# First batch's transform kept in SBUF, weights converted by VectorE, first loads placed by hand

## Chip, core and metric

The kernel runs on one core of a Trainium2 chip. The metric is device time in microseconds (us) of one launch, the median of several runs; lower is better.

## What is computed

Three stages follow one another. `x` has 8 batches of 3072 rows with 256 columns, float32.

```
X = np.fft.rfft(x, axis=1); y = np.fft.irfft(X * (filt_r + 1j * filt_i), n=3072, axis=1)
h = y @ w_in                        # 256 -> 1024, y as 24576 rows
sm = softmax(h); solu = h * sm
ln = (solu - mean) / sqrt(var + 1e-6) * g_ln
z = ln @ w_out                      # 1024 -> 256
h2 = z @ w_in2                      # 256 -> 2048
out = (h2 * sigmoid(1.702 * h2)) @ w_out2    # 2048 -> 256
```

The four weight matrices are float64 in memory and are turned into float32 on the chip.

## The kernel before

**Filter.** The Fourier transform of a batch is two matrix products. In the first (`step1`), rows are taken with a stride of 24, so that a tile has 128 partitions; a batch has 12 such tiles of 128 x 512 (`load_x`, `step1`, `store_a`). The result `a` goes to DRAM (`a_d`). In the second, 32 groups of 96 rows (`NG`) are read back (`load2`: 96 KB of `bt` from `a_d`, 264 KB of `gt` with the group's matrices and filter), multiplied (`forward`, `swap`), filtered (`weigh`), turned back (`inverse`) and stored to DRAM (`z_d`, `store_z`). Batch 0 runs alone through `EarlyFilter`, with one float32 matmul for each product; batches 1 and 2 and later ones run in pairs, mixed into the other stages' work.

**Two layers.** 96 pairs of 128-row tiles go through `First` (filter's last product, 256 -> 1024, softmax, norm, a shuffle through DRAM, 1024 -> 256) and `Second` (256 -> 2048, tanh gate, 2048 -> 256). The first `First` reads `z_d` of batch 0 and so needs all 32 groups of it (`assert filtered[b] == NG`).

**Weights.** 24 parts of 128 x 512 float64 words (512 KB each) are loaded (`Weights.load`) and converted: on VectorE (DVE) `magnitude` (3 instructions), `sign` (1), `lower` (2); on GpSimd (POOL) `add`; on ScalarE (ACT) `scale_rows` for some parts and `split_hi`; on POOL `split_lo`. Fifteen parts (`EARLY["count"]`) are converted along with batch 0's filter, in two buffers (tag "e"); nine (w4's and one more) after it, in three.

**Order.** Nothing is scheduled by the compiler. Each step is put into a list with a time (`at`), the list is sorted, and each engine and the one DMA queue (SyncE, SP) take their instructions in that order; 16 units are one pair. The tables `FIRST`, `SECOND`, `DENSE`, `EARLY` hold the times. An instruction that waits holds up all that stand behind it on its engine, and a DMA issue that waits for a free buffer holds up all later DMA issues.

```
start2 = end - v["gap"] - step2 * NG        # first group of batch 0
start1 = start2 - step1 * N2 / 2            # first step1 of batch 0
steps = (f.load2, f.split_m, f.split_a, f.forward, f.swap, f.weigh, f.split_y, f.inverse, f.store_z)
```

Of the kernel before, what the change touches and what calls it, by code (L numbers as in the profile page):

```python
# [10 lines left out]
F32 = mybir.dt.float32  # L11
F32R = mybir.dt.float32r
# [5 lines left out]
ALU = mybir.AluOpType  # L18
# [5 lines left out]
B, S, D = 8, 3072, 256  # L24
# [12 lines left out]


FIRST = {
    "load": -18.49,  # L40
    "y": -15.7,
    "y_lo": -15.4,
    "hidden": ((-13.6, -11.51), (-5.09, -3.6)),
    "top": (-10.5, -2.4),
    "exp": (-9.6, -1.76),
    "weigh": (-8.86, -1.07),
    "square": (-7.25, 0.3),
    "norm": (-6.23, 0.53),
    "shuffle": (-5.5, 1.2),
    "gather": (-4.48, 1.94),  # L50
    "turn": (-1.56, 6.83),
    "u_hi": (-0.97, 7.3),
    "u_lo": (-0.15, 8.0),
    "project": ((9.4, 10.4), (11.4, 12.1)),
    "x2_hi": 12.78,
    "x2_lo": 13.6,
}
# [1 line left out]
SECOND = {  # L59
    "tanh": 0.7,  # L60
    "gate": 1.19,
    "split_hi": 2.42,
    "split_lo": 3.19,
    "output": 4.6,
    "finish": 5.0,
    "store": 6.2,
}


# [7 lines left out]
DENSE = {  # L77
    "start": 15.65,
    "slots": (0.77, 4.65, 8.65, 12.36),
    "second": (-6.99, -2.67, -1.85, -0.07, 0.61, 5.46, 7.59, 10.78, 11.33),  # L80
}

EARLY = {
    "end": -37.0,
    "step1": 0.99,
    "step2": 1.04,
    "gap": 3.8,
    "first": (-2.8, -2.1, 0.0, 0.5),
    "second": (0.7, 1.6, 1.0, 2.8, 2.95, 3.1, 3.35, 4.6, 5.3),
    "direct": 20,  # L90
    "wide": 8,
    "count": 15,
    "between": 4,
    "ahead": ((0.5, 1.6), (1.4, 1.5)),
    "weights": ((-0.7, 1.6), (-3.5, 4.0)),
    "weight": ((-4.9, -2.9, -1.5, -0.6, 0.2, 1.4, 1.8, 2.4), (-1.7, -1.6, -0.6, -0.4, 0.6, 0.9, 1.6, 1.8)),
}


# [88 lines left out]
def fft_filter_solu_gelu(  # L188
# [62 lines left out]
    def split_pair(k, n, name):  # L251
        hi = cst.tile([P, k, n], F32R, name=f"{name}_hi")
        lo = cst.tile([P, k, n], F32R, name=f"{name}_lo")
        return hi, lo
# [1 line left out]
    w1 = split_pair(2, FF1, "w1")  # L256
    w2 = split_pair(K1, D, "w2")
    w3 = split_pair(2, FF2, "w3")
    w4 = split_pair(K2, D, "w4")

    staged = []

    class Weights:


        def __init__(self, n, dst, src, gain, k0, kn, c0, cn):
            self.hi, self.lo = (t[:, k0:k0 + kn, c0:c0 + cn] for t in dst)
            self.shape = [P, kn, cn]
            k, c = slice(k0, k0 + kn), slice(c0, c0 + cn)
            self.half = dst is w4  # L270
            if gain is None:
                self.src = [(slice(0, P), src.rearrange("(k p) n -> p k n", p=P)[:, k, c])]
            else:
                self.src = [
                    (part, rows.rearrange("(k f) n -> f k n", f=Q)[:, k, c])
                    for part, rows in (blocks(src, b) for b in range(P // Q))]
            self.n, self.gain, self.k0 = n, gain, k0

        def load(self):
            if self.n < EARLY["count"]:  # L280
                self.raw = p2.tile(self.shape, U64, tag="e", name="wst")
            else:

                if self.n == EARLY["count"]:
                    staged.append(p1.tile([P, 3, 512], U64, tag="x2", name="wst"))
                self.raw = staged[0][:, self.n % 3].rearrange("p (k n) -> p k n", k=self.shape[1])
            for part, src in self.src:
                dma(out=self.raw[part], in_=src)

# [30 lines left out]
                op0=ALU.mult, op1=ALU.mult)  # L320

        def add(self):
            nc.gpsimd.tensor_tensor(self.f, self.f, self.top.bitcast(F32), op=ALU.add)
            self.f = self.f.rearrange("p (k n) -> p k n", k=self.shape[1])

        def scale_rows(self):
# [13 lines left out]
                        out=self.f[:, k], in_=self.f[:, k], func=AF.Copy, scale=g)  # L340

        def split_hi(self):
            nc.scalar.copy(out=self.hi, in_=self.f)

        def split_lo(self):
            nc.gpsimd.tensor_tensor(self.lo, self.f, self.hi, op=ALU.subtract)

    def weight_parts():
        n = 0
# [16 lines left out]
    def at(t, fn, *args):  # L366
        plan.append((t, len(plan), fn, args))

    def in_order(*times):
        assert all(a < b for a, b in zip(times, times[1:])), times  # L370
# [13 lines left out]
    filtered = [0] * B  # L384

    class Filter:
        pools = {"gt": [(p3, "gt")], "bt": [(p3, "bt")]}

        def __init__(self, batches):
            b0, self.nb = batches[0], len(batches)  # L390
# [15 lines left out]
        def load_x(self, i0):  # L406
            b, i = divmod(i0, N2 // 2)
            xv = x[self.batches[b]].rearrange("(m q) d -> m (q d)", q=N2)
            if self.batches[0] == 0 and i0 < EARLY["wide"]:

                if i0 == 0:
                    self.wide = p1.tile([N1, EARLY["wide"], 2 * D], F32, tag="u", name="xin")
                xt = self.wide[:, i0]
            else:
                xt = p2.tile([N1, 2 * D], F32, tag="xin", name="xin")
            dma(out=xt, in_=xv[:, i * 2 * D:(i + 1) * 2 * D])
            self.x[i0] = xt
# [5 lines left out]
        def step1(self, i):  # L423
            f = ps_m.tile([N1, 2 * D], F32, tag="m", name="f1")
            if i < self.direct:
                nc.tensor.matmul(f, dft1_sb[:, 0], self.x.pop(i), start=True, stop=True)
            else:
                product(f, (fwd1[:, 0], fwd1[:, 1]), self.x.pop(i))
            self.a[i] = p2.tile([N1, 2 * D], F32, tag="az", name="a")
            nc.scalar.copy(out=self.a[i], in_=f)  # L430

        def store_a(self, i):
            b, j = divmod(i, N2 // 2)
            av = self.a_d[b].rearrange("g r d -> (g r d)").rearrange("(s f) -> s f", s=N1)
            dma(out=av[:, j * 2 * D:(j + 1) * 2 * D], in_=self.a.pop(i))
            self.stored += 1

        def load2(self, g):
            assert self.stored == self.steps
            bt = self.tile("bt", g, [R, self.nb, D], F32)  # L440
            dma(out=bt, in_=self.a_d[:, g].rearrange("b r d -> r b d"))
            gt = self.tile("gt", g, [R, 2 * R + 2 * D], F32)
            dma(out=gt, in_=groups[:, g])
            fl = gt[:, 2 * R:].rearrange("p (t n) -> p t n", t=2)
            both = [R, self.nb, D]
            self.t[g] = dict(
                bt=bt, m=gt[:, :2 * R],
                fr=fl[:, 0:1].to_broadcast(both), fi=fl[:, 1:2].to_broadcast(both))

        def split_m(self, g):  # L450
# [48 lines left out]
    class EarlyFilter(Filter):  # L499


        pools = {"gt": [(p3, "gt")], "bt": [(p3, "bt")] * 3 + [(p2, "xs")] * 2}
        wide_gt = None

        def tile(self, name, g, shape, dtype):
# [40 lines left out]
        def inverse(self, g):  # L546
            v = self.t[g]
            f = ps_m.tile([R, self.nb, D], F32, tag="m", name="f3")
            nc.tensor.matmul(f, v["m"][:, R:], v["pr"], start=True, stop=True)
            v["z"] = p2.tile([R, self.nb, D], F32, tag="az", name="z")  # L550
            nc.scalar.copy(out=v["z"], in_=f)

    def plan_filter(batches, first, second):

        f = Filter(batches) if batches[0] else EarlyFilter(batches)
        for i in range(f.steps):
            in_order(*first(i))
            for t, step in zip(first(i), (f.load_x, f.split_x, f.step1, f.store_a), strict=True):
                at(t, step, i)
        for g in range(NG):  # L560
            steps = (
                f.load2, f.split_m, f.split_a, f.forward, f.swap, f.weigh, f.split_y, f.inverse,
                f.store_z)
            t = second(g)
            in_order(t[0], *t[2:])
            in_order(t[0], t[1], t[3])
            for t, step in zip(second(g), steps, strict=True):
                at(t, step, g)

# [276 lines left out]
    for k, block in enumerate(BLOCKS):  # L848
# [4 lines left out]
    start2 = end - v["gap"] - step2 * NG  # L853
    start1 = start2 - step1 * N2 / 2
    plan_filter(
        together[0], lambda i: [start1 + step1 * i + d for d in v["first"]],
        lambda g: [start2 + step2 * g + d for d in v["second"]])

    def dense(g):
        p, k = divmod(g, len(DENSE["slots"]))  # L860
# [2 lines left out]
    def ahead(i):  # L863
        (a, b), (c, d) = v["ahead"]
        n = v["between"]
        t = start2 + a + b * i if i < n else end + c + d * (i - n)
        return [t + dt for dt in v["first"]]

    plan_filter(together[1], ahead, dense)
    for batches in together[2:]:  # L870
# [4 lines left out]
        def second(g):  # L875

            t = piece(len(batches) * N2 // 2 + 4 * (g // 2) + g % 2)
            return [t + d for d in FILTER["second"]]

        plan_filter(batches, lambda i: [piece(i - 4) + d for d in FILTER["first"]], second)  # L880
    for i, w in enumerate(weight_parts()):
        (a, b), (c, d) = v["weights"]
        n = EARLY["count"]
        t = start1 + a + b * i if i < n else end + c + d * (i - n)
        steps = (
            w.load, w.magnitude, w.sign, w.lower, w.add, w.scale_rows, w.split_hi, w.split_lo)
        in_order(*v["weight"][i < n])
        for d, step in zip(v["weight"][i < n], steps, strict=True):
            at(t + d, step)
# [43 lines left out]
```

## Time and profile before

| what | us |
|---|---|
| median of 3 runs | 3744.72 (3741.65 to 3746.28) |
| profiled execution, its own time | 3743.48 |
| span of its trace | 3741.6 |
| first load of x issued, from the span's start | 3.57 |
| first load of `bt` issued | 51.67 |
| last store of batch 0's `z_d` issued | 148.78 |
| first matmul of `Second` (L765) | 248.50 |

The span runs from the first to the last recorded instruction. PE is TensorE's matmul row, PEld its weight loads, SPq the issuing of DMAs on SyncE's queue. "DMA share" is the mean busy share of the core's 16 DMA engines. In the chain of waits, a piece "DMA x<-y" is time in which the next instruction waited for that transfer.

### The profile page before, as it was taken

The numbers are of one execution on the slowest core, as the hardware profiler recorded it, in microseconds if no ns is written. First come the engines' busy times: TensorE is split into PE (matmuls) and PEld (weight loads), VectorE is DVE, ScalarE is ACT, GpSimd is POOL, SyncE is SP. The second block draws the span as 40 slices with busy tenths as digits, with TensorE's granted clock in tenths as the row PEclk, the third lists the DMA queues.
The fourth block names the chain that finished last, engine by engine and source line by source line (L and its number), as shares of the span: only waits on it lengthen the run. The fifth ranks groups of instructions, "written<-read, shape, count | busy, mean of one in ns | idle before, by whom it ended". The sixth has DMA issues, their size and how long they took to land.

```text
span 3741.6 us, 53627 instructions
## 1 busy us (share of the span) xinstructions
PE 3633.5 (97%) x18304; PEld 3017.0 (81%) x18304; DVE 2691.7 (72%) x3825; ACT 1998.7 (53%) x3570; POOL 860.0 (23%) x1397
## 2 busy tenths in 40 slices
PE   5779999999999999999999999999999999999999
PEld 2368888888888888888888888888888888888888
DVE  8658887667777777666777777667777776766675
ACT  2246665555555555555555555555555554544453
POOL 4333332222222221222222222122222221111110
PEclk6889999999999999999999999999999999999999
DMA  7745554334434443343434343433333332222321
GB/s 225 229 149 152 149 151 123 124 121 114 115 114 114 116 119 104 124 135 108 118 111 122 109 118 112 115 110 102 107 110 106 101 107 86 76 80 72 87 74 32
DMA packets 385683, 433.93 MB, mean 116 GB/s; under 512 B 144128, under 2 KB 294784, under 8 KB 385408
## 3 DMA queue, kind: packets, MB, share of 16 engines
q1 hardware_dynamic: 385408, 430.49, 39.6%
q8 instruction: 145, 2.38, 0.3%
q14 instruction: 130, 1.06, 0.1%
HBM read 232.13 MB, written 176.16 MB: 109 GB/s over the span
## 4 chain that ended last, share of the span: by engine, by line
PE 83%; DVE 7%; DMA 3%; issue 3%; POOL 1%; ACT 1%; SPq 1%; DVEq 0%; POOLq 0%; ACTq 0%
PE h L765 24%; PE o L804 24%; PE x L706 15%; PE h L624 12%; PE f L382 5%; PE yt L606 2%; DVE e L649 1%; DVE u L696 1%; DVE th L777 1%; SPq L827 1%; DMA wst<-in_w_in 1%; POOL mt L454 1%; DVE ob L815 1%; DMA xw<-xs 1%; DMA e_d<-e 0%
## 5 line engine op out<-in xcount | busy, mean ns | idle before, releaser
L765 PE MATMUL h<-x2s,w_hi 128*128 128x512 f32 (+1 forms) x3136 | 956.5, 387 | 0.0
L783 ACT CAST gh<-th 128x512 fp32r<-128x512 f32 x768 | 474.2, 617 | 465.1 <-DVE th L777 386.3
L777 DVE SCALAR_TENSOR_TENSOR th<-th,h 128x512 f32<-128x512 f32 x768 | 523.8, 682 | 246.0 <-ACT th L772 242.8
L789 DVE TENSOR_TENSOR gl<-th,gh 128x512 fp32r<-128x512 f32 x768 | 534.6, 696 | 194.7 <-ACT gh L783 192.2
L765 PEld LDWEIGHTS h<-x2s,w_hi 128*128 128x128 f32 x3136 | 571.7, 189 | 107.6
L772 ACT ACTIVATE th<-h 128x512 f32<-128x512 f32 x768 | 457.5, 596 | 335.2 <-PE h L765 334.7
L706 PE MATMUL x<-u,w_hi 128*128 128x256 f32 x3072 | 622.9, 285 | 11.6 <-DVE u L696 10.5
L804 PE MATMUL o<-gh,w_hi 128*128 128x512 f32 (+1 forms) x1568 | 615.9, 393 | 2.0 <-DVE ob L815 1.7
L804 PE MATMUL o<-gl,w_hi 128*128 128x512 f32 (+1 forms) x1568 | 607.4, 387 | 0.0
L804 PE MATMUL o<-gh,w_lo 128*128 128x512 f32 (+1 forms) x1568 | 606.6, 387 | 0.0
L706 PEld LDWEIGHTS x<-u,w_hi 128*128 128x128 f32 x3072 | 505.8, 192 | 37.2 <-DVE u L696 18.8
L765 PE MATMUL h<-x2s,w_lo 128*128 128x512 f32 (+1 forms) x1568 | 478.3, 386 | 0.0
L706 PE MATMUL x<-u,w_lo 128*128 128x256 f32 x1536 | 435.8, 284 | 0.0
L636 ACT ACTIVATE e<-h,nmx 128x1024 f32<-128x1024 f32 x192 | 214.6, 1117 | 326.1 <-DVE nmx L630 309.9
L804 PEld LDWEIGHTS o<-gl,w_hi 128*128 128x128 f32 x1568 | 295.0, 188 | 68.9 <-DVE gl L789 9.6
L804 PEld LDWEIGHTS o<-gh,w_hi 128*128 128x128 f32 x1568 | 296.1, 189 | 63.8 <-issue 11.0
L765 PEld LDWEIGHTS h<-x2s,w_lo 128*128 128x128 f32 x1568 | 292.8, 188 | 62.5
L804 PEld LDWEIGHTS o<-gh,w_lo 128*128 128x128 f32 x1568 | 296.1, 189 | 51.0
L640 POOL TENSOR_SCALAR q<-se 128x1 f32<-128x1 f32 x192 | 44.1, 230 | 1204.8 <-ACT e L636 1204.7
L706 PEld LDWEIGHTS x<-u,w_lo 128*128 128x128 f32 x1536 | 294.6, 192 | 14.9
L669 DVE TENSOR_SCALAR e<-e,nmu,rs 128x1024 f32<-128x1024 f32 x192 | 160.8, 837 | 179.8 <-POOL rs L664 177.4
L649 DVE SCALAR_TENSOR_TENSOR e<-h,e 128x1024 f32<-128x1024 f32 x192 | 232.2, 1209 | 33.3 <-ACT e L636 20.7
(82 smaller groups left out, 5303.0 us busy)
## 6 DMA issues: line engine op xcount, KB each, us to landing
e_d<-e SPq DMA_DIRECT2D x192, 512.0 KB, 2.6
e<-e_d SPq DMA_DIRECT2D x768, 128.0 KB, 3.0
gt<-in_groups SPq DMA_DIRECT2D x160, 264.0 KB, 3.8
xin<-in_x SPq DMA_DIRECT2D x96, 256.0 KB, 3.3
a_d<-a SPq DMA_DIRECT2D x96, 256.0 KB, 2.3
zr<-z_d SPq DMA_DIRECT2D x96, 256.0 KB, 3.3
out<-ob SPq DMA_DIRECT2D x768, 32.0 KB, 1.6
bt<-a_d SPq DMA_DIRECT2D x96, 192.0 KB, 3.5
```

Of the source, the lines that this page charges most:

```text
L382: nc.tensor.matmul(out, w[i], x[j], start=m == 0, stop=m == 2)
L624: nc.tensor.matmul(hs, xx[:, c, a * P:(a + 1) * P], ww[:, c, f * 512:(f + 1) * 512], start=(m == 0 and c == 0), stop=(m == 2 and c == 1))
L636: nc.scalar.activation(out=e, in_=self.h[a], func=AF.Exp, bias=self.v[a], accum_out=se)
L649: nc.vector.scalar_tensor_tensor(out=e, in0=self.h[a], scalar=1.0, in1=e, op0=ALU.mult, op1=ALU.mult, accum_out=su)
L669: nc.vector.tensor_scalar(out=e, in0=e, scalar1=nmu, scalar2=rs, op0=ALU.add, op1=ALU.mult)
L706: nc.tensor.matmul(self.x2[:, c], ww[:, kk, c * P:(c + 1) * P], uu[:, kk], start=(c == 0 and kk == 0 and m == 0), stop=(kk == K1 - 1 and m ...
L765: nc.tensor.matmul(self.part(t, j), ww[:, c, f * P:(f + 1) * P], xx[..., c, :], start=(m == 0 and c == 0), stop=(m == 2 and c == 1))
L772: nc.scalar.activation(out=th, in_=self.t[d], func=AF.Tanh, scale=0.851)
L777: nc.vector.scalar_tensor_tensor(out=self.g[d], in0=self.g[d], scalar=1.0, in1=self.t.pop(d), op0=ALU.add, op1=ALU.mult)
L783: nc.scalar.copy(out=gh, in_=self.g[d])
L789: nc.vector.tensor_tensor(gl, th, gh, op=ALU.subtract)
L804: nc.tensor.matmul(o, ww[:, f, h * P:(h + 1) * P], self.part(gg, j), start=(f == 0 and m == 0), stop=(f == K2 - 1 and m == 2))
```

## The change

- The 12 tiles of batch 0's x are loaded first, with three weight parts among them, into one tile `x0` of 24 KB per partition, which takes the place in SBUF that w4's converted weights take later. `step1` writes its result back into `x0`; `store_a` does nothing for batch 0.
- `load2` falls into `load_gt` and `load_bt`. For batch 0 `load_bt` copies SBUF to SBUF: 24 rows of 1 KB from each of the four partitions `4g` to `4g+3` to the 96 partitions of `bt`. `load_gt` of the first eight groups stands earlier, beside `step1`.
- `add` and `split_lo` of the weights go from POOL to DVE.
- Weight parts 0 to 14 use five buffers instead of two; each load has a time of its own (`loads`).
- Batch 0's `z` has six buffers instead of two.
- Some times in `FIRST`, `SECOND` and `DENSE` move by up to about one unit.

```diff
 EARLY = {
     "end": -37.0,
-    "step1": 0.99,
-    "step2": 1.04,
-    "gap": 3.8,
-    "first": (-2.8, -2.1, 0.0, 0.5),
-    "second": (0.7, 1.6, 1.0, 2.8, 2.95, 3.1, 3.35, 4.6, 5.3),
+    "step1": 0.73,
+    "step2": 0.95,
+    "gap": 2.88,
+    "x": (-3.0, 0.1),
+    "gt": (-0.01, 1.11),
+    "first": (-2.1, 0.0, 0.5),
+    "second": (0.3, 0.31, 1.19, 1.3, 2.52, 2.82, 3.47, 4.1, 4.6, 5.3),
...
+    "loads": (-81.75, -81.7, -81.86, -77.86, -75.86, -73.86, -71.86, -69.86, -67.86, -65.86, -63.86, -61.86, -59.86, -57.86, -55.86, -46.4, -42.4, -38.4, -34.96, -30.4, -26.12, -22.4, -18.4, -16.17),
-    "weights": ((-0.7, 1.6), (-3.5, 4.0)),
+    "weights": ((1.12, 1.9), (-3.5, 4.0)),
...
+    x0 = p1.tile([N1, N2 // 2, 2 * D], F32, tag="w4", name="x0")
...
-            if self.n < EARLY["count"]:
+            if self.n < EARLY["count"] and self.n % 5 > 2:
                 self.raw = p2.tile(self.shape, U64, tag="e", name="wst")
             else:
...
-                self.raw = staged[0][:, self.n % 3].rearrange("p (k n) -> p k n", k=self.shape[1])
+                self.raw = staged[0][:, STAGE[self.n]].rearrange("p (k n) -> p k n", k=self.shape[1])
...
         def add(self):
-            nc.gpsimd.tensor_tensor(self.f, self.f, self.top.bitcast(F32), op=ALU.add)
+            nc.vector.tensor_tensor(self.f, self.f, self.top.bitcast(F32), op=ALU.add)
...
         def split_lo(self):
-            nc.gpsimd.tensor_tensor(self.lo, self.f, self.hi, op=ALU.subtract)
+            nc.vector.tensor_tensor(self.lo, self.f, self.hi, op=ALU.subtract)
...
-            self.a[i] = p2.tile([N1, 2 * D], F32, tag="az", name="a")
+            if self.batches[0] == 0:
+
+                nc.scalar.copy(out=x0[:, i], in_=f)
+                self.stored += 1
+                return
+            self.a[i] = self.tile("az", i, [N1, 2 * D], F32)
             nc.scalar.copy(out=self.a[i], in_=f)
 
         def store_a(self, i):
+            if self.batches[0] == 0:
+                return
...
+        def load_bt(self, g):
             assert self.stored == self.steps
             bt = self.tile("bt", g, [R, self.nb, D], F32)
-            dma(out=bt, in_=self.a_d[:, g].rearrange("b r d -> r b d"))
+            if self.batches[0] == 0:
+                dma(out=bt[:, 0],
+                    in_=x0[4 * g:4 * g + 4].rearrange("s a (b d) -> s (a b) d", d=D))
+            else:
+                dma(out=bt, in_=self.a_d[:, g].rearrange("b r d -> r b d"))
...
-        pools = {"gt": [(p3, "gt")], "bt": [(p3, "bt")] * 3 + [(p2, "xs")] * 2}
+        pools = {
+            "gt": [(p3, "gt")], "bt": [(p3, "bt")] * 3 + [(p2, "xs")] * 2,
+            "az": [(p2, "az"), (p2, "fh"), (p2, "fl")] * 2}
...
+        lambda g: (
+            start1 + v["gt"][0] + v["gt"][1] * g if g < 8
+            else start2 + step2 * g + v["second"][0]))
```

## Rows read from the trace of the kernel before

**Rows 1.** The page, busy share of each engine, then 40 slices.
```profile
PE 3633.5 (97%) x18304; PEld 3017.0 (81%) x18304; DVE 2691.7 (72%) x3825; ACT 1998.7 (53%) x3570; POOL 860.0 (23%) x1397
PE   5779999999999999999999999999999999999999
```

**Rows 2.** Busy time by stage: us of stretch, us and count by engine.
```profile
core 0: us, PE busy (x) PEld busy (x) DVE busy (x) ACT busy (x) POOL busy (x), PEclk, DMA share, GB/s
0.00:51.70 51.70, 26.12 (x28) 7.14 (x28) 40.47 (x53) 15.55 (x30) 20.35 (x20) 0.66 0.75 232
51.70:149.00 97.30, 68.79 (x200) 36.33 (x198) 77.31 (x147) 18.75 (x45) 37.76 (x81) 0.74 0.75 217
149.00:300.00 151.00, 114.88 (x537) 86.48 (x536) 89.56 (x124) 69.48 (x128) 53.49 (x68) 0.83 0.56 173
300.00:3700.00 3400.00, 3389.38 (x17304) 2855.12 (x17305) 2466.67 (x3475) 1881.10 (x3348) 748.38 (x1228) 1.00 0.38 110
```

**Rows 3.** Chain of waits from 0 to 149 us, share by line.
```profile
by line: DMA wst<-in_w_in 16.1%; DMA gt<-in_groups 10.4%; DVE w_top L310 7.9%; DVE w_mag L301 7.4%; issue 6.1%; PE f L549 6.1%; PE f L525 5.9%; DVE w_mag L299 5.4%; PE f L532 5.1%; DVE w_mag L318 3.7%; DMA xin<-in_x 3.5%; DVE w_wt L316 2.9%
```

**Rows 4.** Timeline, SP queue: first loads, first bt, last z store.
```profile
3.57 0.45 SPq L416 DMA_DIRECT2D xin<-in_x  x1
4.06 0.43 SPq L288 DMA_DIRECT2D wst<-in_w_in  x1
...
51.67 0.34 SPq L441 DMA_DIRECT2D bt<-a_d  x1
...
148.78 0.32 SPq L495 DMA_DIRECT2D z_d<-z  x1
```

**Rows 5.** DMA issues, 0 to 149 us: count, KB each, us to landing.
```profile
gt<-in_groups SPq DMA_DIRECT2D x32, 264.0 KB, 4.1
wst<-in_w_in SPq DMA_DIRECT2D x12, 512.0 KB, 5.5
xin<-in_x SPq DMA_DIRECT2D x18, 256.0 KB, 4.1
a_d<-a SPq DMA_DIRECT2D x16, 256.0 KB, 3.8
bt<-a_d SPq DMA_DIRECT2D x32, 96.0 KB, 3.5
z_d<-z SPq DMA_DIRECT2D x32, 96.0 KB, 3.0
```

**Rows 6.** Timeline of the weights' conversion on DVE and POOL.
```profile
9.16 0.43 DVE L299 TENSOR_SCALAR w_mag<-wst 128x512 int32<-128x512 int32 x1 [5.73 <-DMA wst<-in_w_in]
9.62 0.43 DVE L301 TENSOR_SCALAR w_mag<-w_mag 128x512 f32<-128x512 f32 x1
10.55 0.69 DVE L310 SCALAR_TENSOR_TENSOR w_top<-wst,w_mag 128x512 int32<-128x512 int32 x1
...
12.51 1.38 POOL L323 TENSOR_TENSOR w_mag<-w_mag,w_top 128x512 f32<-128x512 f32 x1 [11.69 <-DVE w_mag L318]
...
17.53 0.42 DVE L299 TENSOR_SCALAR w_mag<-wst 128x512 int32<-128x512 int32 x1
17.98 1.37 DVE L301 TENSOR_SCALAR w_mag<-w_mag 128x512 f32<-128x512 f32 x1
19.85 1.76 DVE L310 SCALAR_TENSOR_TENSOR w_top<-wst,w_mag 128x512 int32<-128x512 int32 x1
22.71 0.42 DVE L299 TENSOR_SCALAR w_mag<-wst 128x512 int32<-128x512 int32 x1
```

**Rows 7.** Groups of instructions: L789 of the whole run, the rest 0 to 149 us.
```profile
L789 DVE TENSOR_TENSOR gl<-th,gh 128x512 fp32r<-128x512 f32 x768 | 534.6, 696 | 194.7 <-ACT gh L783 192.2
...
L541 DVE TENSOR_TENSOR pr<-pr,xw 96x256 f32<-96x256 f32 x32 | 16.4, 513 | 1.0
L535 DVE SCALAR_TENSOR_TENSOR xw<-f,sgn_sb,gt 96x256 f32<-96x256 f32 x32 | 15.3, 477 | 3.5 <-PE f L532 3.1
L527 DVE TENSOR_TENSOR pr<-f,gt 96x256 f32<-96x256 f32 x32 | 13.4, 418 | 10.5 <-PE f L525 10.5
...
L551 ACT COPY z<-f 96x256 f32<-96x256 f32 x32 | 11.8, 368 | 65.9 <-PE f L549 42.3 <-DMA z_d<-z 23.7
```

**Rows 8.** Timeline, SP queue: three DMAs that run with no other.
```profile
234.88 0.34 SPq L676 DMA_DIRECT2D e_d<-e  x1
...
905.97 0.30 SPq L495 DMA_DIRECT2D z_d<-z  x1
...
2028.19 0.51 SPq L474 DMA_DIRECT2D xw<-xs  x1
```

**Rows 9.** Busy time over those three transfers, then over a full stretch.
```profile
235.70:237.15 1.45, 1.45 (x5) 1.26 (x6) 0.95 (x2) 0.47 (x1) 0.00 (x0) 0.50 0.91 362
906.78:907.75 0.97, 0.97 (x6) 0.76 (x5) 0.37 (x1) 0.91 (x2) 0.00 (x0) 1.00 0.74 200
2029.35:2029.90 0.55, 0.55 (x6) 0.51 (x5) 0.55 (x1) 0.55 (x2) 0.55 (x1) 1.00 0.65 179
...
20.00:52.00 32.00, 17.48 (x18) 4.68 (x18) 30.07 (x37) 11.19 (x23) 15.84 (x12) 0.50 0.82 251
```

More of the change, by code (lines that the diff above doesn't have):

```diff
@@ L39 @@
 FIRST = {
-    "load": -18.49,
+    "load": -18.75,
     "y": -15.7,
     "y_lo": -15.4,
-    "hidden": ((-13.6, -11.51), (-5.09, -3.6)),
+    "hidden": ((-13.6, -11.24), (-4.04, -3.7)),
     "top": (-10.5, -2.4),
[L45 to L49, printed above, removed]
+    "exp": (-9.6, -1.69),
+    "weigh": (-8.86, -1.19),
+    "square": (-8.15, 0.3),
+    "norm": (-6.68, 0.43),
+    "shuffle": (-5.5, 0.95),
     "gather": (-4.48, 1.94),
-    "turn": (-1.56, 6.83),
+    "turn": (-1.56, 6.89),
     "u_hi": (-0.97, 7.3),
     "u_lo": (-0.15, 8.0),
-    "project": ((9.4, 10.4), (11.4, 12.1)),
+    "project": ((9.4, 10.02), (11.4, 12.1)),
     "x2_hi": 12.78,
@@ L61 @@
     "gate": 1.19,
-    "split_hi": 2.42,
+    "split_hi": 2.47,
     "split_lo": 3.19,
-    "output": 4.6,
+    "output": 4.92,
     "finish": 5.0,
-    "store": 6.2,
+    "store": 6.61,
 }
@@ L79 @@
     "slots": (0.77, 4.65, 8.65, 12.36),
-    "second": (-6.99, -2.67, -1.85, -0.07, 0.61, 5.46, 7.59, 10.78, 11.33),
+    "second": (-6.78, -2.67, -1.85, -0.07, 0.61, 5.46, 7.59, 10.89, 10.96),
 }
+STAGE = [i % 5 if i < 15 else i % 3 for i in range(24)]
 EARLY = {
     "end": -37.0,
-    "step1": 0.99,
-    "step2": 1.04,
-    "gap": 3.8,
-    "first": (-2.8, -2.1, 0.0, 0.5),
-    "second": (0.7, 1.6, 1.0, 2.8, 2.95, 3.1, 3.35, 4.6, 5.3),
+    "step1": 0.73,
[5 more added lines that the diff above has]
+    "second": (0.3, 0.31, 1.19, 1.3, 2.52, 2.82, 3.47, 4.1, 4.6, 5.3),
+    "more": (-2.8, -1.5, 0.0, 0.5),
     "direct": 20,
-    "wide": 8,
     "count": 15,
     "between": 4,
-    "ahead": ((0.5, 1.6), (1.4, 1.5)),
-    "weights": ((-0.7, 1.6), (-3.5, 4.0)),
-    "weight": ((-4.9, -2.9, -1.5, -0.6, 0.2, 1.4, 1.8, 2.4), (-1.7, -1.6, -0.6, -0.4, 0.6, 0.9, 1.6, 1.8)),
+    "ahead": ((0.5, 1.45), (1.4, 1.5)),
+    "loads": (-81.75, -81.7, -81.86, -77.86, -75.86, -73.86, -71.86, -69.86, -67.86, -65.86, -63.86, -61.86, -59.86, -57.86, -55.86, -46.4, -42.4, -38.4, -34.96, -30.4, -26.12, -22.4, -18.4, -16.17),
+    "weights": ((1.12, 1.9), (-3.5, 4.0)),
+    "weight": ((-2.92, -0.81, -0.6, 0.2, 1.29, 1.8, 3.49), (-1.28, -1.05, -0.4, 0.51, 0.79, 1.6, 1.8)),
 }
@@ L258, in fft_filter_solu_gelu @@
     w3 = split_pair(2, FF2, "w3")
-    w4 = split_pair(K2, D, "w4")
+    x0 = p1.tile([N1, N2 // 2, 2 * D], F32, tag="w4", name="x0")
+    w4 = []
     staged = []
@@ L266, in __init__ @@
         def __init__(self, n, dst, src, gain, k0, kn, c0, cn):
-            self.hi, self.lo = (t[:, k0:k0 + kn, c0:c0 + cn] for t in dst)
+            self.dst = dst, slice(k0, k0 + kn), slice(c0, c0 + cn)
             self.shape = [P, kn, cn]
@@ L279, in load @@
         def load(self):
-            if self.n < EARLY["count"]:
+            if self.n < EARLY["count"] and self.n % 5 > 2:
                 self.raw = p2.tile(self.shape, U64, tag="e", name="wst")
             else:
-                if self.n == EARLY["count"]:
+                if not staged:
                     staged.append(p1.tile([P, 3, 512], U64, tag="x2", name="wst"))
-                self.raw = staged[0][:, self.n % 3].rearrange("p (k n) -> p k n", k=self.shape[1])
+                self.raw = staged[0][:, STAGE[self.n]].rearrange("p (k n) -> p k n", k=self.shape[1])
             for part, src in self.src:
@@ L342, in split_hi @@
         def split_hi(self):
+            dst, k, c = self.dst
+            if not dst:
+                t = p1.tile([P, 2, K2, D], F32R, tag="w4", name="w4")
+                dst.extend(t[:, i] for i in range(2))
+            self.hi, self.lo = (t[:, k, c] for t in dst)
             nc.scalar.copy(out=self.hi, in_=self.f)
         def split_lo(self):
-            nc.gpsimd.tensor_tensor(self.lo, self.f, self.hi, op=ALU.subtract)
+            nc.vector.tensor_tensor(self.lo, self.f, self.hi, op=ALU.subtract)
     def weight_parts():
@@ L386, in fft_filter_solu_gelu @@
     class Filter:
-        pools = {"gt": [(p3, "gt")], "bt": [(p3, "bt")]}
+        pools = {"gt": [(p3, "gt")], "bt": [(p3, "bt")], "az": [(p2, "az")]}
         def __init__(self, batches):
@@ L408, in load_x @@
             xv = x[self.batches[b]].rearrange("(m q) d -> m (q d)", q=N2)
[L409 to L413, printed above, removed]
+            if self.batches[0] == 0:
+                xt = x0[:, i0]
             else:
@@ L438, in load2, with load_gt @@
         def load2(self, g):
+            self.load_gt(g)
+            self.load_bt(g)
+        def load_bt(self, g):
             assert self.stored == self.steps
             bt = self.tile("bt", g, [R, self.nb, D], F32)
-            dma(out=bt, in_=self.a_d[:, g].rearrange("b r d -> r b d"))
+            if self.batches[0] == 0:
+                dma(out=bt[:, 0],
+                    in_=x0[4 * g:4 * g + 4].rearrange("s a (b d) -> s (a b) d", d=D))
+            else:
+                dma(out=bt, in_=self.a_d[:, g].rearrange("b r d -> r b d"))
+            self.t[g]["bt"] = bt
+        def load_gt(self, g):
             gt = self.tile("gt", g, [R, 2 * R + 2 * D], F32)
@@ L446, in load2 @@
             self.t[g] = dict(
-                bt=bt, m=gt[:, :2 * R],
+                m=gt[:, :2 * R],
                 fr=fl[:, 0:1].to_broadcast(both), fi=fl[:, 1:2].to_broadcast(both))
@@ L549, in inverse, with plan_filter @@
             nc.tensor.matmul(f, v["m"][:, R:], v["pr"], start=True, stop=True)
-            v["z"] = p2.tile([R, self.nb, D], F32, tag="az", name="z")
+            v["z"] = self.tile("az", self.steps + g, [R, self.nb, D], F32)
             nc.scalar.copy(out=v["z"], in_=f)
-    def plan_filter(batches, first, second):
+    def plan_filter(batches, first, second, early=None):
         f = Filter(batches) if batches[0] else EarlyFilter(batches)
@@ L561, in plan_filter @@
             steps = (
-                f.load2, f.split_m, f.split_a, f.forward, f.swap, f.weigh, f.split_y, f.inverse,
-                f.store_z)
+                f.load_bt if early else f.load2, f.split_m, f.split_a, f.forward, f.swap, f.weigh,
+                f.split_y, f.inverse, f.store_z)
             t = second(g)
@@ L568, in plan_filter @@
                 at(t, step, g)
+            if early:
+                in_order(early(g), second(g)[1])
+                at(early(g), f.load_gt, g)
     def segments(start, count):
@@ L855, in fft_filter_solu_gelu @@
     plan_filter(
-        together[0], lambda i: [start1 + step1 * i + d for d in v["first"]],
-        lambda g: [start2 + step2 * g + d for d in v["second"]])
+        together[0],
+        lambda i: [start1 + v["x"][0] + v["x"][1] * i] + [
+            start1 + step1 * i + d for d in v["first"]],
+        lambda g: [start2 + step2 * g + d for d in v["second"][1:]],
+        lambda g: (
+            start1 + v["gt"][0] + v["gt"][1] * g if g < 8
+            else start2 + step2 * g + v["second"][0]))
     def dense(g):
@@ L866, in ahead @@
         t = start2 + a + b * i if i < n else end + c + d * (i - n)
-        return [t + dt for dt in v["first"]]
+        return [t + dt for dt in v["more"]]
     plan_filter(together[1], ahead, dense)
@@ L885, in fft_filter_solu_gelu @@
         steps = (
-            w.load, w.magnitude, w.sign, w.lower, w.add, w.scale_rows, w.split_hi, w.split_lo)
+            w.magnitude, w.sign, w.lower, w.add, w.scale_rows, w.split_hi, w.split_lo)
+        in_order(v["loads"][i], t + v["weight"][i < n][0])
+        at(v["loads"][i], w.load)
         in_order(*v["weight"][i < n])
```

## The prediction

> **What bounds the kernel now.** I read the page first. TensorE (PE) is busy 97% of the span, and only the first slices of its row fall short of nine tenths [rows 1]. The busy time by stage says the same in us: from 300 to 3700 us PE has 3389 of 3400, so at most 11 us are to be had there; of the first 300 us it lacks 90 [rows 2]. The edits that can matter all lie before 149 us, when the last group of batch 0 is stored and the first pair may begin [rows 4]. So the question is when that store comes; what follows it moves with it, since `First` waits for all 32 groups and the queues keep their order.
>
> The chain of waits up to 149 us has no single owner: loads of weights and of `gt` together 26%, DVE's conversion lines (L299 to L318) 27%, the matmuls of the groups about 17% [rows 3]. Two resources are nearly full: DVE, 117.8 of 149 us busy, and the DMA engines, busy share 0.75 throughout, 0.82 at 251 GB/s from 20 to 52 us [rows 2, 9]. I take 251 GB/s as what this stage's ordinary mix of loads and stores can get.
>
> **The weights on DVE.** A part now takes 5.18 us of DVE, from one L299 to the next (17.53 to 22.71); L301 takes 1.37 us and L310 1.76 us while a POOL instruction runs, 0.43 and 0.69 us when none does [rows 6]. After the edit a part has four instructions of 0.43, two of 0.69 and two more of 128x512, for which I take the 0.70 of L789, which also reads two SBUF tiles [rows 7]; with eight gaps of 0.03 that is 4.74 us. The two POOL instructions of 1.3 us leave the part's chain. A group adds L527, L535 and L541, 1.41 us, 1.5 with gaps [rows 7]. Fifteen parts and 32 groups: 15 x 4.74 + 32 x 1.5 = 119 us. DVE starts later than today's 9.16 us: part 0 is fifth in the queue, behind three tiles of x and another part. These five are 1.83 MB, 7.3 us at 251 GB/s; counted from about 5 us, when the first bytes flow, part 0 is there at 12 us. DVE alone would end the groups at 131, and with the last inverse and store at about 134 us. For the nine parts after the groups the gain is 9 x 0.44 = 4 us of DVE, which is busy 90 of 151 us there [rows 2]; I count nothing, 4 us at most.
>
> **x in front and the transform in SBUF.** The loads of x and of the first three parts, 15 issues of 0.45 us, wait for nothing, as their buffers are new: 3.57 + 6.8 = 10.4 us [rows 4]. The copy of `step1`'s result by ACT stays what it was, with another target. Twelve stores of 256 KB to `a_d` go away [rows 5], 3.1 MB or 12.5 us of the DMA engines at 251 GB/s. That `w4` shares its place with `x0` costs nothing while the last copy to `bt` stands some five units ahead of w4's first conversion; if the copies come late, ACT waits there with `First` behind it, which is the same delay once more and not another. Six buffers for `z` take away the 23.7 us that ACT waited for `z_d` stores [rows 7]; worth something only where DMA and DVE are not the bound, so I count nothing beside the sums here.
>
> If a copy to `bt` cost what the load from `a_d` costs, the DMA engines would have, up to the last group, 12 tiles of x (3.1 MB), 32 `gt` (8.7), `bt` and `z` (3.1 each), 18 weight parts (9.4) and batch 1's first tiles (2.1): 29.5 MB, 118 us at 251 GB/s, ending near 123 us. Then DVE's 134 us counts.
>
> **The copies from four partitions.** This step has no like in the trace. `bt` of group g is now read from partitions 4g to 4g+3 alone, 24 KB from each. Three transfers that run with nothing beside them tell what the number of partitions read does [rows 8, 9]. The store of `e` reads 128: 362 GB/s at a share of 0.91, so a busy engine moves 362 / (16 x 0.91) = 24.9 GB/s. The store of `z` reads 96: 200 / (16 x 0.74) = 16.9. The swap reads 48: 179 / (16 x 0.65) = 17.2. With fewer partitions the same engines are busy longer for the same bytes, though the store of `z` goes to DRAM just as that of `e` does; they seem to wait for each other at the reading side. The bounds of one copy of 96 KB: below, the swap's 0.55 us for the same bytes; above, the swap's rate for each partition, 179 / 48 = 3.7 GB/s, times four, which is 15 GB/s or 6.6 us. Between them I take 24.9 GB/s, 3.95 us: in the widest row each engine moves that with eight partitions to serve, four neighbours will hardly give more than eight, and engines that meet there share it.
>
> [...]
>
> Now the sum for the engines that carry these copies. Their queue is served in order, so the terms add. Ahead of the first copy stand 12 tiles of x, parts 0 to 6, eight `gt` and two tiles of batch 1: 9.5 MB, 38 us at 251 GB/s; from 4 us on, 42 us. From there to the last store, at the unhindered rate of 512 KB in 1.45 us [rows 9]: 24 `gt` at 0.75 us, 18; ten weight parts, 14.5; 32 `z` at half of 0.97 us, 15.5; six tiles of batch 1 at 0.73, 4.4: together 52. And 32 copies of 3.95, 126. The end is 42 + 52 + 126 = 220 us, against 149: 71 us later. DVE's 134 us would lie under it, and the relief of DVE would bring nothing. Break-even lies at (149 - 42 - 52) / 32 = 1.7 us a copy.
>
> **The retuned times.** From 300 us on they can give 11 us at most [rows 2]; they add no instruction and no byte. I count nothing, a few us either way.
>
> **Sum.** The profiled execution took 3743.48 us, 1.9 us more than its span and 1.2 under the median. The change adds 71 us: 3814.5 beside the execution, 3816 beside the median of 3744.72.
>
> **Rivals.**
> 1. The other sign: the copies are as cheap as the swap, because four partitions can feed several engines at once. For it: the swap moves 179 GB/s from 48 partitions, and its first bound is 0.55 us. Then 42 + 52 + 18 = 112 us is less than DVE's 134, DVE sets the end, and the time is 3744.7 - 15 = 3730. It decides wherever a copy costs under 1.5 us. Against it: a rate that falls by a third between 128 and 96 partitions does not suggest that four do as well.
> 2. The copies cost between 1.5 and 1.9 us. The front ends where it does now: 3745, give or take 7.
> 3. The front gets 15 us shorter, but the stage up to 300 us keeps its end, since its loads of x for batch 1 and its nine weight parts pace it and not the first pair. Against it: the chain there has to pass through `First`, which waits for the last group; and its DMA share is only 0.56 [rows 2]. Time 3740 to 3748.
>
> **How the numbers follow.** Slow copies: 0.6. Rival 1: 0.28. Rivals 2 and 3 together: 0.12. The forecast is the first: 3816 us. Its own range goes by a copy of 3.0 to 4.8 us, 30 us less and 27 more: 3786 to 3843. The range for 8 in 10 must reach to rival 1 and to its DVE sum: 3728 to 3845; a copy of 6.6 us, which would give 3900, is left out, and so is rival 1 with all 11 us of the steady stage. A change of 0.2%, 7.5 us, is about what a measurement of this kernel tells from none. So slower 0.6, the same 0.12, faster 0.28.
>
> **What the changed profile would show.** If I am right: the DMA issues give `bt<-x0` a time to landing far above the 3.5 us of today [rows 5], some 8 to 20 us with several in the queue; the chain of waits up to the last `z_d` store is led by that transfer; GB/s in the groups' stretch falls to about half of today's 217, with the DMA share near 1 if all 16 engines are held and near a third if only a few are; DVE is idle for half of it; the last `z_d` store comes at about 220 us. In either case L301 and L310 of the weights should fall to 0.43 and 0.69 us, the `step1` matmuls should be done before 40 us instead of 52, and the steady stage should be as before, only shifted. I am wrong if `bt<-x0` lands in 2 to 4 us: then the last store comes near 134 us, DVE is nearly full until then and the time is near 3730. I am wrong in another way if the last store is late with the copies fast, which would put the cause at DVE or in the order of the queues.

## The result and the profile after

The changed kernel took 3794.61 us (median of 4 runs, 3793.83 to 3795.82) against 3743.73 us before: ratio 1.0136, 95% interval 1.0118 to 1.0153, slower by 51 us. The forecast was 3816 us, slower, with 3728 to 3845 as its range.

The stages of the changed kernel, as in [rows 2]; the second row ends with the groups of batch 0:

```profile
core 0: us, PE busy (x) PEld busy (x) DVE busy (x) ACT busy (x) POOL busy (x), PEclk, DMA share, GB/s
0.00:36.60 36.60, 17.25 (x24) 5.64 (x24) 22.31 (x43) 10.78 (x18) 3.75 (x13) 0.77 0.91 242
36.60:205.00 168.40, 101.38 (x206) 51.41 (x206) 89.56 (x198) 26.16 (x61) 14.13 (x56) 0.52 0.51 131
205.00:356.00 151.00, 115.46 (x539) 86.12 (x538) 91.09 (x132) 66.95 (x123) 33.33 (x52) 0.80 0.53 166
356.00:3750.00 3394.00, 3384.25 (x17292) 2853.68 (x17292) 2473.25 (x3475) 1888.28 (x3346) 793.25 (x1228) 1.00 0.38 110
```

The first stage got what it was to get: 242 GB/s at a share of 0.91, and it ends 15 us earlier than before. The second stage is as much longer as to lose that and 51 us more: DVE is busy for little over half of it, and the DMA engines move 131 GB/s where they moved 217. The last two stages are those of before, shifted.

The issues on the queue, as in [rows 4]:

```profile
36.61 0.83 SPq L462 DMA_DIRECT2D bt<-x  x1
...
44.77 2.25 SPq L462 DMA_DIRECT2D bt<-x  x1
...
198.59 1.69 SPq L522 DMA_DIRECT2D z_d<-az  x2
```

The first copy to `bt` is issued 15 us earlier than the load it replaces, the last `z_d` store, at 200 us, 51 us later. The span after that store is 3793.1 - 200.0 = 3593.1 us; before it was 3741.6 - 148.8 = 3592.8. So the whole loss lies between 36 and 200 us.

Who waited there (engine and line, for whom, us in all, times, longest):

```profile
POOL ms L545 <- DMA gt<-in_groups: 117.9, 24, 16.1
ACT az L580 <- PE f L578: 94.6, 25, 5.4
...
DVE pr L556 <- PE f L578: 64.9, 29, 3.7
PE f L554 <- DMA bt<-x: 51.0, 26, 3.4
```

POOL waits for `gt`, PE for `bt`, ACT and DVE for PE. The wait for `gt` is the longest, although `gt` comes from DRAM as before: it stands in the same queue behind the copies, and in the trace of before none of the 2794 transfers landed ahead of one issued earlier. The trace also records when each engine's part of a load lands. Of the 24 `gt` loads of this stretch, the twelfth of 16 parts landed 4.2 us after the issue in the median, the last 6.1 us; before, these were 3.5 and 4.1 us. So four parts of 16 come late, as they would if four engines are behind the other twelve. One stretch in which the engines carry nothing but a copy shows its price:

```profile
108.50:110.50 2.00, 2.00 (x6) 1.11 (x4) 0.50 (x2) 0.37 (x1) 0.38 (x2) 0.50 0.22 24
```

A share of 0.22 is four busy engines of 16 (0.25, less gaps; the trace has four packets on the way for 1.30 of the 2.00 us, and five for 0.01), and together they move 24 GB/s, about the 24.9 that one engine moved in the widest row of [rows 9]. 96 KB at 24 GB/s are 4.1 us. The trace lists every packet, which is here one row of 1 KB moved by one engine: in this stretch 43 of 46 took 152 to 180 ns. The weights' instructions on DVE (count, busy us, mean ns), as in [rows 6, 7]:

```profile
L317 DVE SCALAR_TENSOR_TENSOR w_top<-wst,w_mag 128x512 int32<-128x512 int32 x18 | 12.4, 687 | 0.2
L330 DVE TENSOR_TENSOR w_mag<-w_mag,w_top 128x512 f32<-128x512 f32 x18 | 12.3, 682 | 0.0
...
L308 DVE TENSOR_SCALAR w_mag<-w_mag 128x512 f32<-128x512 f32 x18 | 7.7, 428 | 0.6
```

L308 is L301 of before, now at 0.43 us without the 1.37 us that it took beside POOL; L317 is L310, at 0.69 us; L330 is `add`, now on DVE.

### The profile page after: what moved, and what is told of

The parts are those of the page before. It is cut to its first block, busy times and chain, and to the rows that moved or that the text cites. A ratio compares the mean times of both kernels' runs of the same rounds, so it can differ in the third digit from the quotient of the medians.

```text
span 3793.1 us, 53398 instructions
## 1 busy us (share of the span) xinstructions
PE 3654.6 (96%) x18304; PEld 3030.3 (80%) x18304; DVE 2695.1 (71%) x3873; ACT 2006.6 (53%) x3570; POOL 844.5 (22%) x1349
## 4 chain that ended last, share of the span: by engine, by line
PE 80%; DVE 6%; issue 3%; DMA 2%; POOL 1%; ACT 1%; SPq 1%; DVEq 0%; POOLq 0%; ACTq 0%
PE h L798 24%; PE o L837 23%; PE x L739 15%; PE h L657 12%; PE f L394 5%; PE yt L639 2%; DVE e L682 1%; DVE th L810 1%; DVE u L729 1%; SPq L860 1%; POOL mt L481 1%; DVE ob L848 1%; DMA out<-ob 1%; DMA e_d<-e 0%; DVE gl L822 0%
## 5 line engine op out<-in xcount | busy, mean ns | idle before, releaser
L837 PE MATMUL o<-gh,w 128*128 128x512 f32 (+1 forms) x3136 | 966.4, 390 | 1.9 <-DVE ob L848 1.7
L837 PEld LDWEIGHTS o<-gh,w 128*128 128x128 f32 x3136 | 570.0, 189 | 115.7 <-issue 11.0
L837 PE MATMUL o<-gl,w 128*128 128x512 f32 (+1 forms) x1568 | 606.8, 387 | 0.5 <-DVE gl L822 0.5
L837 PEld LDWEIGHTS o<-gl,w 128*128 128x128 f32 x1568 | 295.1, 188 | 67.4 <-DVE gl L822 7.4
L481 POOL TENSOR_TENSOR mt<-gt,mt 96x192 fp32r<-96x192 f32 x128 | 142.5, 1113 | 502.7 <-ACT mt L480 488.9
L657 PE MATMUL h<-w_hi,xl 128*128 128x512 f32 x768 | 242.2, 397 | 5.4 <-DVE xl L648 5.4
L657 PE MATMUL h<-w_hi,xh 128*128 128x512 f32 x768 | 243.0, 398 | 3.1 <-ACT xh L644 3.1
L663 DVE TENSOR_REDUCE nmx<-h 128x1 f32<-128x1024 f32 x192 | 234.8, 1223 | 15.3 <-PE h L657 7.9
```

Source lines behind the costliest of these rows:

```text
L481: nc.gpsimd.tensor_tensor(mt[:, 1], v["m"], mt[:, 0], op=ALU.subtract)
L657: nc.tensor.matmul(hs, xx[:, c, a * P:(a + 1) * P], ww[:, c, f * 512:(f + 1) * 512], start=(m == 0 and c == 0), stop=(m == 2 and c == 1))
L663: nc.vector.tensor_reduce(out=nmx, in_=self.h[a], op=ALU.max, axis=AX.X, negate=True)
L837: nc.tensor.matmul(o, ww[:, f, h * P:(h + 1) * P], self.part(gg, j), start=(f == 0 and m == 0), stop=(f == K2 - 1 and m == 2))
```

## Experiments

Theory A: four neighbouring partitions give all engines that read them together the stream of one, and the engines that carry the 32 copies set the end of the groups. Rivals: the DVE work added to each weight part (B), the new order in the queue (C), the mere number of partitions (A2). Ratios are to the kernel before, timed on the same chip.

| label | what | us | ratio, 95% | last z store |
|---|---|---|---|---|
| e1_dram | `bt` through DRAM | 3734.84 | 0.9974 (0.9965 to 0.9984) | 140.4 |
| e2_96part | copies read 96 partitions | 3730.7 | 0.9962 (0.9946 to 0.9977) | 136.4 |
| e3_apart | rows 4 partitions apart | 3733.87 | 0.9974 (0.9964 to 0.9984) | 138.6 |
| e4_twice | each copy twice | 3982.59 | 1.0636 (1.0614 to 1.0657) | 388.5 |
| e5_before_dve | before, weights on DVE | 3745.22 | 1.0003 (0.9993 to 1.0013) | 146.8 |
| e6_apart_pool | e3, weights on POOL | 3737.65 | 0.9984 (0.9975 to 0.9993) | 142.6 |
| e7_32apart | rows 32 partitions apart | 3739.02 | 0.9985 (0.9974 to 0.9995) | 142.1 |
| e8_after_pool | changed, weights on POOL | 3797.4 | 1.0141 (1.0121 to 1.0161) | 201.5 |
| e11_apart_again | e3 again | 3732.64 | 0.9971 (0.996 to 0.9983) | 143.0 |
| e12_apart_pool_again | e6 again | 3737.32 | 0.9978 (0.997 to 0.9987) | 141.9 |
| e9_apart_dve3 | e3, `sign` twice | 3739.62 | 0.9985 (0.9977 to 0.9994) | 144.8 |
| e10_apart_z2 | e3, two buffers for z | 3735.82 | 0.9977 (0.9967 to 0.9986) | 143.0 |

In all of them the span after the last `z_d` store is 3592 to 3597 us. The store's time is of the one profiled execution; the time is a median. The same kernel, as e3 and as e11, has its store at 138.6 and at 143.0 us, so a few us between two of these times say nothing.

**Copies undone.** e1 keeps the rest of the change, with the loads in front, the five weight buffers and the weights on DVE, and takes only the copies back:

```diff
         def store_a(self, i):
             if self.batches[0] == 0:
-                return
+                self.a[i] = x0[:, i]
...
-            if self.batches[0] == 0:
-                dma(out=bt[:, 0],
-                    in_=x0[4 * g:4 * g + 4].rearrange("s a (b d) -> s (a b) d", d=D))
-            else:
-                dma(out=bt, in_=self.a_d[:, g].rearrange("b r d -> r b d"))
+            dma(out=bt, in_=self.a_d[:, g].rearrange("b r d -> r b d"))
```

> The changed kernel, with batch 0's transform written to a_d again and each bt read from there (12 stores of 256 KB come back); all else as changed. Theory A (reading four neighbouring partitions gives four engines together the stream of one, 4 us a copy, and these engines set the end of the groups): the last z_d store comes near 135 to 140 us instead of 200, time 3730 to 3738. Rival B (the two more DVE instructions of each weight part set the end): no change, 3790 to 3800. Rival C (the new order of loads in the one queue sets the end): no change, 3790 to 3800.

3734.84 us: the loss is gone and 9 us of gain appear. B and C fall.

**Same bytes, more partitions.**

```diff
-                    in_=x0[4 * g:4 * g + 4].rearrange("s a (b d) -> s (a b) d", d=D))
+                    in_=x0[:R, g % 12, :D])
```

> The changed kernel, but each copy to bt takes its 96 KB from 96 partitions of x0 (1 KB each) and not from four, so bt holds other values and the output is not the filter's. Bytes, issues, waits and order stay. Theory A: a copy takes about 0.55 us on all engines, the last z_d store comes near 135 us, time 3728 to 3735. Rivals B and C: 3790 to 3800.

3730.7 us. Nothing differs from the changed kernel but where the 96 KB are read, and with it, perhaps, how many engines carry them; that is worth 64 us. Which of the two it is, this run does not tell.

**Number or place.** A column order of the first matrix that puts a group's four rows four partitions apart:

```diff
+    fwd0 = cst.tile([N1, N1], F32, name="fwd0")
+    nc.vector.tensor_copy(
+        out=fwd0.rearrange("p (u j v) -> p u j v", u=8, v=4),
+        in_=dft1_sb[:, 0].rearrange("p (u v j) -> p u j v", u=8, v=4))
...
-                    in_=x0[4 * g:4 * g + 4].rearrange("s a (b d) -> s (a b) d", d=D))
+                    in_=x0[g // 4 * 16 + g % 4:g // 4 * 16 + 16:4].rearrange(
+                        "s a (b d) -> s (a b) d", d=D))
```

> The changed kernel with the columns of batch 0's first matrix in another order, so that the four rows of a group lie in partitions four apart (16u+v, +4, +8, +12) instead of side by side; the result is the same. Still four partitions, 96 KB, 24 rows of 1 KB each. Theory A with the outlet being a block of four neighbouring partitions: each engine has its own, 24 rows of 46 ns, a copy takes 1.1 us, the four engines need 39 + 52 + 35 = 126 us and DVE's 134 us sets the end: time 3728 to 3736. Rival A2 (the price goes by the number of partitions read or of engines used, wherever they lie): no change, 3790 to 3800. Rivals B and C: the same, 3790 to 3800.

3733.87 us. Four partitions, and a quarter of the engines, are enough when the partitions lie four apart; A2 falls. A stretch of e3 with little but a copy in it, and the stretch of its groups:

```profile
93.00:93.75 0.75, 0.75 (x3) 0.33 (x2) 0.72 (x2) 0.37 (x1) 0.00 (x1) 0.50 0.26 87
36.00:138.60 102.60, 82.67 (x201) 42.68 (x202) 83.26 (x189) 24.08 (x56) 23.36 (x56) 0.63 0.74 210
```

A quarter of the engines now moves 87 GB/s and not 24; most rows in the first stretch took 46 ns. e7 takes `x0[g::32]`, with `fwd0` ordered to match:

> The changed kernel with the columns of batch 0's first matrix in another order, so that the four rows of a group lie 32 partitions apart (g, g+32, g+64, g+96); the result is the same. [...]

3739.02 us. A stretch of e7:

```profile
61.10:61.70 0.60, 0.60 (x3) 0.46 (x2) 0.60 (x3) 0.00 (x0) 0.00 (x0) 0.50 0.24 43
```

43 GB/s by a quarter of the engines, about half of e3's 87, and most rows took 84 to 87 ns, where e3's took 46. That is 2.3 us a copy, against 1.1 in e3 and 4.1 in the changed kernel. Its price in time, 5 us over e3 with intervals that overlap, is smaller than the 37 us that 32 copies of 1.16 us more would make; that the engines had that much room is likely, not shown.

**The cost doubled.**

```diff
-                dma(out=bt[:, 0],
-                    in_=x0[4 * g:4 * g + 4].rearrange("s a (b d) -> s (a b) d", d=D))
+                for _ in range(2):
+                    dma(out=bt[:, 0],
+                        in_=x0[4 * g:4 * g + 4].rearrange("s a (b d) -> s (a b) d", d=D))
```

> The changed kernel with each copy to bt issued twice into the same tile. Theory A: 32 more copies of 4 us on the same engines, 100 to 128 us more, time 3895 to 3925. Rivals B and C: 32 more issues of some 0.5 us, mostly hidden: under 20 us more, 3795 to 3815.

3982.59 us, 188 us more: 5.9 us for each second copy, beyond the 4 us of A and far beyond B and C. The two copies write one tile, and the queue holds the second until the first has landed (who waited, for whom, us in all, times, longest):

```profile
SPq L463 <- DMA bt<-x: 167.7, 32, 6.3
```

A stretch with a copy alone:

```profile
154.50:156.25 1.75, 0.00 (x0) 0.00 (x0) 0.00 (x0) 0.00 (x0) 0.00 (x0) 0.50 0.22 23
```

The price of a copy alone is nearly the same, 23 GB/s. The expectation left that wait of the queue out, and the 1.8 us beyond 4.1 are put down to it. So this run confirms the direction and the price from the row, not the size.

**The weights on DVE.** Three kernels change `nc.gpsimd` to `nc.vector` in `add` and `split_lo`, or back: e5 on the kernel before (there `magnitude` also moves 0.25 units later), e8 on the changed one, e6 on e3.

> The kernel before, with add and split_lo of the weights on DVE and nothing else of the change (magnitude of a part stands 0.25 units later, behind split_lo of the part two before it). By the prediction's sum a part costs DVE 4.74 us instead of 5.18, 15 x 0.44 = 6.6 us up to the last group, of which DVE's share of the chain (a quarter) is 2 us, at most all: the last z_d store at 142 to 148 us, time 3737 to 3744. Rival (POOL was free help, and eight instructions of a part on one engine delay the groups' DVE work): slower by 5 to 15 us, 3749 to 3759.

> The changed kernel with add and split_lo back on POOL, copies from four neighbours as changed. Theory A (engines that carry the copies set the end, so the relief of DVE brings nothing): the same within 4 us, 3790 to 3799. Rival (DVE still counts on the path): 3799 to 3805.

> The kernel with the four rows of a group four partitions apart, and add and split_lo back on POOL. Theory D (with cheap copies DVE sets the end of the groups, as the prediction's rival 1 has it): 5 to 8 us slower than with DVE, last z_d store 143 to 147 us, time 3738 to 3743. Theory M (the DMA engines set it, DVE has room): the same within 3 us, 3731 to 3737.

e5: 1.0003 (0.9993 to 1.0013), nothing, though 7 us of DVE's busy time are saved. e8: 3 us over the changed kernel, too little to tell from it. e6: 4 us over e3, with intervals that overlap; so e3 and e6 were timed again side by side on one chip, with two more kernels.

> The kernel with a group's four rows four partitions apart, once more, beside the three that follow: 3731 to 3737.

> The same with add and split_lo on POOL, once more beside it. Theory D (DVE sets the end of the groups when the copies are cheap): 3 to 7 us slower than with DVE. Theory M (DMA engines and waits for gt set it, DVE has room): within 2 us of it.

> The kernel with rows four apart, and the DVE instruction of sign issued twice in every weight part (the second writes the same values again), 0.72 us more of DVE for each of 16 or 17 parts before the last group, 12 us in all. Theory D: the last z_d store 9 to 12 us later, 3742 to 3747. Theory M: under 4 us later, 3732 to 3739.

```diff
-            nc.vector.scalar_tensor_tensor(
-                out=self.top, in0=self.high, scalar=-0x40000000, in1=self.mag,
-                op0=ALU.bitwise_and, op1=ALU.bitwise_or)
+            for _ in range(2):
+                nc.vector.scalar_tensor_tensor(
+                    out=self.top, in0=self.high, scalar=-0x40000000, in1=self.mag,
+                    op0=ALU.bitwise_and, op1=ALU.bitwise_or)
```

e12 is 4.7 us over e11, its interval again overlapping. e9 adds 12 us of DVE and its median is 7 us over e11's, between theory D and theory M; here too the intervals overlap, and its last store came only 1.8 us after e11's. All three medians point to DVE as part of the bound when the copies are cheap, not as the whole of it, but none of them shows it. In the row of e3's groups above DVE is busy 83 of 103 us and the DMA share is 0.74.

> The kernel with rows four apart, and two buffers for batch 0's z instead of six. By the prediction (the waits of ACT for z_d stores are worth nothing where DMA and DVE are the bound): within 3 us, 3731 to 3738. Rival (those waits, 23.7 us before, are where the groups' pace came from): 8 to 20 us slower, 3741 to 3755.

```diff
-            "az": [(p2, "az"), (p2, "fh"), (p2, "fl")] * 2}
+            "az": [(p2, "az")]}
```

e10: 3 us over e11, inside both intervals, although ACT waits 35.3 us for `z_d` stores again. So with cheap copies such waits cost at most a few us; the 23.7 us in [rows 7] are likely no more of a loss.

## Why the prediction was right, and where its sizes were off

- **What bounds.** Right. All that moved lies before the last `z_d` store, and 3592 to 3597 us follow it in every kernel. The retuned times gave nothing that can be seen: 3593.1 us after the store against 3592.8. The forecast's own range, 3786 to 3843 us, holds the measured time too; the range of 3728 to 3845 also held the other sign.
- **The copy's price.** Right: 3.95 us forecast, 4.1 us measured at 24 GB/s. The reason given, that engines which meet at neighbouring partitions share one engine's stream, agrees with the runs: the four moved 24 GB/s together; e3 moves only the place of the rows, to four apart, they move 87, and 61 us go; 32 apart (e7) they move 43. What it is that such partitions share, no run shows. The reading of [rows 9] behind it does not hold: four partitions as such do not slow an engine. In e3 a busy engine moves 87 / (16 x 0.26) = 21 GB/s from four partitions, more than the 16.9 and 17.2 that were read for 96 and 48. To take the 24.9 between bounds of 0.55 and 6.6 us was in part luck.
- **The sum of the engines.** Right in its form, 20 us too long. The term that was mis-sized is "32 copies of 3.95, 126". From the first copy to the last store the forecast had 52 + 126 = 178 us; the trace has 200.0 - 36.6 = 163.4. The price of 3.95 us fits a copy alone, whose rows took 152 to 180 ns, and in the mix at most half of the rows took that long: of the 3072 rows copied no more than 1509 took 150 ns or longer. That for the others the four engines did not read at once is likely, not shown. All packets of 1 KB in the stretch, copies and `z_d` stores, took 534 us together. The stores were 2965 of the 6037; at no less than 44 ns each, the shortest time there, they took 130 us or more. That leaves at most 404 us for the copies, 101 us for each of the four engines and 3.2 us a copy. Everything in the stretch took 0.51 x 163.4 x 16 = 1333 us of engine time; less the copies, spread over 16, that is 58 us an engine, where the forecast had 52. So the four engines come to at most 101 + 58 = 159 us of work in 163. The terms do add, as the prediction said (of the 2750 transfers of the changed kernel with all 16 parts in the trace none landed ahead of one issued earlier), and fill nearly all of the time. That the rest is spread evenly is assumed, not shown. The other 5 us are the start: the first copy was issued at 36.6 us and not 42.
- **DVE.** The price of a part was right: its instructions took 0.43 and 0.69 us. That its relief would bring nothing under slow copies agrees with e8, as far as its two executions tell.
- **Rival 1.** It gave 3730 us for cheap copies; with the price removed the kernel takes 3731 to 3735 (e2, e1, e3). So its number was right, its condition was not met. Its reason, that DVE sets the end, is not shown and at most half so (e9: 7 us for 12), so the number fits in part by luck. And by its own sum DVE sets the end only below (134 - 42 - 52) / 32 = 1.25 us a copy, not 1.5; e3's copies lie below both.
- **What the profile was to show.** GB/s in the groups' stretch fell to 131, not to half of 217; the share is 0.51, more than "near a third", since the other engines were not idle. By the landings in the trace a copy took 6.2 to 9.5 us from issue to landing, 7.7 in the median: far above 3.5, a little below the "8 to 20". The chain of waits does not answer whether the copies lead it, since it breaks off at 191.9 us. DVE was idle for half of the stretch, as forecast (84.7 of 163.4 us busy). The first 15 issues took until 15.2 us and not 10.4, so they did not run unhindered.

What gives the 9 to 13 us of gain in e1, e3 and e11 was not taken apart. It is not the weights on DVE alone (e5), not the six buffers of z (e10), and not staying in SBUF, as e1 stores and reloads `a` and is as fast as e3. That leaves the loads in front, the early `gt`, the five weight buffers and the new times of the groups, untested one by one.

## What to carry to other kernels

A transfer inside SBUF is not cheap because it avoids DRAM: here the way through DRAM (e1) took 3734.84 us and the copies 3794.61. Look at which partitions one DMA reads. Four neighbours gave here 24 GB/s where four partitions that lie four apart gave 87, and the price falls on the transfers behind it in the queue: the last part of a `gt` load landed after 6.1 us in the median and not 4.1, that of a `z_d` store after 5.9 and not 3.0. A different order of rows, made in a constant, removed it, and e3, with the same result, takes 0.9971 to 0.9974 of the time of the kernel before. And when one event (here the last `z_d` store) has a nearly constant remainder behind it, its time tells where a loss lies. It is no finer a ruler than the median: it is one execution's, and e3 and e11, the same kernel, differ by 4.4 us. Last, a price read while one transfer runs alone need not be its price in the mix: the copies cost 4.1 us alone and at most 3.2 on average.

## What the runs showed of the hardware that was not expected

- A copy from four partitions ran on a quarter of the 16 engines, by a share of 0.22 (neighbours), 0.26 (four apart) and 0.24 (32 apart). In the changed kernel four of the 16 parts of a load came late: twelve parts of a `gt` load landed after 4.2 us in the median, the last after 6.1.
- Most rows of 1 KB took 46 ns when a copy's four partitions lay four apart (e3), 84 to 87 ns when they lay 32 apart (e7), and 152 to 180 ns when they were neighbours (the changed kernel).
- The issue of a copy itself took longer where the copies were slow: 0.66 to 3.70 us in the changed kernel, 0.66 to 0.88 in e3.
